# Second products gathered in six PSUM banks, the next pair's operands made in the first products, and the keys' maxima transposed behind the second products

## The chip, the cores and the metric

The kernel runs on 1 core of one Trainium2 chip. The metric is the device time of one execution in microseconds (us); the time given is the median of three runs.

## The reference, cut to what matters

```python
q_s = softmax of q over each row of 64          # 8 batches x 8 heads x 576 x 64
k_s = softmax of k over the sequence (axis 2)   # needs each column's maximum over 576 rows
kv  = einsum('bhsd,bhse->bhde', k_s, v)
x   = einsum('bhsd,bhde->bhse', q_s, kv)        # seen as 4608 tokens x 512
h   = x @ w_in                                  # 512 -> 2048
x   = (h * clip(h + 3, 0, 6) / 6) @ w_out       # first MLP, 2048 -> 512
h   = x @ w2_in
out = (h * sigmoid(h)) @ w2_out                 # second MLP, the same sizes
```

Everything is fp32. Each fp32 operand of a product is split into an upper and a lower fp32r part, and a product is the sum of three TensorE products (upper x upper, upper x lower, lower x upper).

## The kernel before, in words

The 4608 tokens are 9 blocks of 512 (NB). **Attention and the first MLP** run together, block by block. Each block has 16 steps (f = 0 to 15). A step `n` issues on TensorE `mm1(s)` (12 matmuls, the hidden block h), small attention matmuls, and `mm2(prev)` (12 matmuls of the step before). One attention unit (two heads of a block) begins every four steps and goes through stages 0 to 6; of its keys, stage 0 takes maxima over five row groups on VectorE (`k_max`, three instructions, L290 to L292), stage 1 transposes them on TensorE (`k_turn`, L297) and reduces them on VectorE (`k_peak`, L303), stage 2 spreads the result over the partitions (`k_spread`, L309). `q_load` brings the transposed queries back through DRAM (`zd`) on ScalarE's DMA queue. In these steps each engine works in the order in which the code emits; there is no scheduler.

**The second MLP** treats blocks 1 to 8 as four pairs (b = 0 to 3); block 0 is done at the very end with plain `mm1`/`mm2`. A pair is computed by a Strassen-like scheme with seven products P1 to P7 in place of eight, once for the *first products* (x times w2_in, function `inner`, L992) and once for the *second products* (gated hidden times w2_out, function `outer`, L1142). A unit is 6 matmuls of 128x128 by 512 columns. The first products of a pair are 56 units, P1 to P7 for each of 8 hidden pairs n, each hidden pair gathered in three PSUM banks A, B and C. The second products are 56 units too, product by product in the order of `KEYS`, 8 units (i = 0 to 7) each. Their moving operands come from the gated hidden tiles `g` and sums of them: GpSimd makes T1 and T3 while the first products run, and T2 and T4 while the second run (`next_t2`, `next_t4`); ScalarE takes the upper part (`split`, L1081), VectorE the lower (`split_low`, written by the helper at L979), `LOOK` = 4 units ahead into one of five rotating tile pairs (`split_tile`). `joins` adds the products into eight kept tiles `fixed`, from which `turn` transposes the output during the next pair's first products. Banks are handed out in rotation over eight (`bank`).

Two blocks' x operands for the next pair are prepared by `x_ahead`, in two column halves c: four loads of 256 KB from `yd`, sums on GpSimd, seven splits (`high` on ScalarE, `low` on VectorE) whose parts are stored to `xd`. `x_fetch` reads them back into the operand tiles during the second products. Weights come through six `ring` tiles of two units each, fetched six tiles ahead by `fetch` (L878).

The order of the second MLP is a table of events: `when(t, fn)` files a piece of code at time t, in units, and the pieces are emitted in the order of t. So t decides the place in each engine's queue, and nothing else: an engine runs the next instruction of its queue as soon as what it waits for is there.

Of the kernel before, what the change touches and what calls it, by code (L numbers as in the profile page):

```python
# [9 lines left out]
F32 = mybir.dt.float32  # L10
# [18 lines left out]
def efficient_attention_then_two_mlps(  # L29
# [47 lines left out]
    xd = dram.tile([2, 7, P, 2, 2, BLK], F32, name="xd")  # L77
# [80 lines left out]
    OUTER = ("A11", "S3", "S2", "S1", "S4", "A22", "A12")  # L158
# [800 lines left out]
    KEYS = ("P1", "P7", "P6", "P5", "P3", "P4", "P2")  # L959

    def second_mlp(last):
# [48 lines left out]
        def pair_events(b, n, t):  # L1010
# [37 lines left out]
            def t3():  # L1048
                add(op["spare"][:, n], g_of(2 * n + 1)[:, 1], g_of(2 * n)[:, 1],
                    ALU.subtract, nc.gpsimd)  # L1050
# [15 lines left out]
        def split_tile():  # L1066
            n = turns[0] % 5
# [29 lines left out]
        def x_ahead(j, c, side, t, step):  # L1097

            st = {n: op["spare"][:, 3 + m] for m, n in enumerate(("B12", "B22", "B11", "B21", "T"))}

            def load(n):
                jj, h = j + (n[2] == "2"), int(n[1] == "2")
                nc.sync.dma_start(st[n], yd[jj, 2 * h + c])

            def high(n, src):
                d["x", n] = split_tile()
                nc.scalar.copy(d["x", n][0], st[src])  # L1107

            def low(n, src):
                hi, lo = d.pop(("x", n))  # L1110
                add(lo, st[src], f32(hi), ALU.subtract)
                to = xd[side, XS.index(n)]
# [333 lines left out]
```

## Time and profile before

| | |
|---|---|
| median of 3 runs (lowest, highest) | 1659.18 us (1657.49, 1660.66) |
| the profiled execution: its time, its span | 1661.98 us, 1660.3 us |
| TensorE matmul busy | 1613.2 us, 97% |
| VectorE, ScalarE, GpSimd busy | 1075.3, 740.2, 422.4 us |
| DMA traffic, mean over the span | 317.61 MB, 191 GB/s |
| mean granted TensorE clock | 0.997 of full |

The span is the time from the first to the last instruction of the profiled execution; 1.68 us of the execution's time lie outside it. A TensorE matmul's busy time overlaps the next one's, so how long a run of matmuls takes is read from the starts.

### The profile page before, as it was taken

How to read it: one execution, taken by the hardware profiler on the slowest of the kernel's cores; microseconds unless marked ns; L12 is line 12 of the kernel's file. 1: busy time of each engine (PE TensorE's matmuls, PEld its weight loads, DVE VectorE, ACT ScalarE, POOL GpSimd, SP SyncE). 2: the span in 40 equal slices, each digit the busy share in tenths (PEclk: the TensorE clock that was granted, in tenths of full speed). 3: DMA queues.
4: the chain of work that ended last, by engine and by line, in shares of the span. 5: the costliest groups of instructions: out<-in, count | busy, mean ns of one | idle time of the engine just before them, and what ended most of it. 6: DMA issues, size and time to landing. Idle time of an engine off the chain costs nothing.

```text
span 1660.3 us, 22032 instructions
## 1 busy us (share of the span) xinstructions
PE 1613.2 (97%) x7612; PEld 1302.0 (78%) x7612; DVE 1075.3 (65%) x1737; ACT 740.2 (45%) x1306; POOL 422.4 (25%) x334
## 2 busy tenths in 40 slices
PE   6999999999999999999999899999999999999998
PEld 4777787787877788888888687788778878887887
DVE  8996666565666666555556568865976595569422
ACT  6885344343444444443434344444444443444322
POOL 2100111101111110111121456343724370345000
PEclk9999999999999999999999899999999999999999
DMA  8912434444543434443341977987899687669730
GB/s 252 337 35 67 132 105 140 123 137 130 168 122 106 138 116 141 129 138 98 93 161 58 335 285 282 361 310 237 297 349 310 222 302 256 216 213 356 241 127 26
DMA packets 291838, 317.61 MB, mean 191 GB/s; under 512 B 113424, under 2 KB 197392, under 8 KB 291728
## 3 DMA queue, kind: packets, MB, share of 16 engines
q1 hardware_dynamic: 228768, 300.97, 53.9%
q10 hardware_dynamic: 62960, 15.25, 4.1%
q8 instruction: 60, 0.98, 0.2%
q14 instruction: 50, 0.41, 0.1%
HBM read 234.62 MB, written 81.53 MB: 190 GB/s over the span
## 4 chain that ended last, share of the span: by engine, by line
PE 64%; DVE 17%; ACT 6%; DMA 6%; issue 4%; ACTq 3%; POOL 0%; SPq 0%; DVEq 0%; POOLq 0%
PE pb L992 17%; PE h L493 17%; PE y L563 14%; PE pb L1142 10%; DVE gsp L979 6%; ACTq L424 3%; PE y L565 2%; DMA zd<-qz 2%; DMA xd<-gsp 2%; DVE r L513 2%; PE pa L451 1%; ACT g L521 1%; ACT r L506 1%; DVE fa L128 1%; DVE fa L132 1%
## 5 line engine op out<-in xcount | busy, mean ns | idle before, releaser
L493 PE MATMUL h<-x,wi 128*128 128x512 f32 x1920 | 472.6, 393 | 2.4 <-DVE wi L153 1.0
L563 PE MATMUL y<-g,wo 128*128 128x512 f32 x1728 | 420.6, 392 | 0.0
L493 PEld LDWEIGHTS h<-x,wi 128*128 128x128 f32 x1920 | 356.6, 188 | 79.3 <-DVE wi L153 2.7
L563 PEld LDWEIGHTS y<-g,wo 128*128 128x128 f32 x1728 | 321.3, 188 | 67.0
L992 PE MATMUL pb<-xo,ring 128*128 128x512 f32 x1344 | 317.1, 394 | 8.4 <-DVE U L979 6.8
L1142 PE MATMUL pb<-gsp,ring 128*128 128x512 f32 x1344 | 316.5, 393 | 6.1 <-DVE gsp L979 3.4
L1142 PEld LDWEIGHTS pb<-gsp,ring 128*128 128x128 f32 x1344 | 249.6, 188 | 71.7 <-DVE gsp L979 18.1
L992 PEld LDWEIGHTS pb<-xo,ring 128*128 128x128 f32 x1344 | 252.3, 189 | 62.1 <-DVE U L979 7.2
L513 DVE SCALAR_TENSOR_TENSOR r<-r,h 128x512 f32<-128x512 f32 x128 | 88.0, 687 | 209.5 <-ACT r L506 204.5
L979 DVE TENSOR_TENSOR gsp<-g,gsp 128x512 fp32r<-128x512 f32 x192 | 169.3, 906 | 45.2 <-ACT gsp L1081 44.1
L1081 ACT CAST gsp<-g 128x512 fp32r<-128x512 f32 x192 | 115.3, 621 | 110.1 <-PE pb L1142 52.9
L506 ACT ACTIVATE r<-h 128x512 f32<-128x512 f32 x144 | 86.2, 599 | 152.5 <-PE h L493 133.7
L521 ACT CAST g<-r 128x512 fp32r<-128x512 f32 x144 | 89.5, 622 | 118.7 <-DVE r L513 106.6
L524 DVE TENSOR_TENSOR g<-r,g 128x512 fp32r<-128x512 f32 x144 | 103.9, 722 | 53.6 <-ACT g L521 43.8
L398 POOL TENSOR_TENSOR qe<-qe,qs 128x512 f32<-128x512 f32 x36 | 37.7, 1046 | 345.5 <-DVE qs L393 332.2
L979 DVE TENSOR_TENSOR g<-r,pb 128x512 f32<-128x512 f32 x96 | 65.6, 683 | 54.3 <-ACT r L1005 54.1
L979 DVE TENSOR_TENSOR gsp<-spare,gsp 128x512 fp32r<-128x512 f32 x74 | 83.9, 1163 | 18.0 <-ACT gsp L1107 18.0
L376 POOL TENSOR_TENSOR qe<-qraw,qm 128x512 f32<-128x512 f32 x34 | 36.0, 1060 | 215.1 <-DVE qm L368 139.4
L1005 ACT ACTIVATE r<-pb 128x512 f32<-128x512 f32 x96 | 57.1, 595 | 75.3 <-DVE pb L979 63.2
L979 POOL TENSOR_TENSOR s<-U,s 128x512 f32<-128x512 f32 x32 | 43.5, 1359 | 154.5 <-DVE U L979 83.3
L197 POOL TENSOR_TENSOR ws_sum<-fa 128x256 f32<-128x256 f32 x32 | 29.4, 920 | 163.7 <-ACT r L506 96.2
L354 ACT ACTIVATE kv<-pa,rs 64x64 fp32r<-64x64 f32 x56 | 17.3, 309 | 108.1 <-DMA qt<-zd 53.6
(152 smaller groups left out, 1640.0 us busy)
## 6 DMA issues: line engine op xcount, KB each, us to landing
ring<-ws SPq DMA_DIRECT2D x224, 512.0 KB, 4.9
ws<-sp SPq DMA_DIRECT2D x128, 256.0 KB, 2.5
xd<-gsp SPq DMA_DIRECT2D x84, 256.0 KB, 5.6
xo<-xd SPq DMA_DIRECT2D x42, 512.0 KB, 6.2
yd<-o SPq DMA_DIRECT2D x36, 256.0 KB, 2.4
wi_early<-in_moe_w_in_dram SPq DMA_DIRECT2D x16, 512.0 KB, 9.3
wo_early<-in_moe_w_out_dram SPq DMA_DIRECT2D x16, 512.0 KB, 9.6
wi_raw<-in_moe_w_in_dram SPq DMA_DIRECT2D x16, 512.0 KB, 4.2
```

What stands on the lines that cost most here:

```text
L424: nc.scalar.dma_start(t[b * 32 : b * 32 + 32].rearrange("i (c a k) -> i c a k", c=NCH, a=4), zb[b])
L493: nc.tensor.matmul(h, w[:, a, c, :], x[:, e, c, :], start=(c == 0 and n == 0), stop=(c == NC - 1 and n == 2),)
L506: nc.scalar.activation(self.r, self.h, AF.Relu, bias=3.0)
L513: nc.vector.scalar_tensor_tensor(out=r, in0=r, scalar=6.0, in1=h, op0=ALU.min, op1=ALU.mult)
L521: nc.scalar.copy(self.g[:, 0], self.r)
L524: nc.vector.tensor_tensor(out=self.g[:, 1], in0=self.r, in1=f32(self.g[:, 0]), op=ALU.subtract)
L563: nc.tensor.matmul(y[c], w[:, a, cs], g[:, e, :], start=st, stop=sp)
L979: (eng or nc.vector).tensor_tensor(out=out, in0=a, in1=b, op=how)
L992: nc.tensor.matmul(to, ws_[:, a], e[:, c], start=p in ("P1", "P6", "P5") and c == 0 and m == 0, stop=c == 1 and m == 2, skip_group_check=True,
L1005: nc.scalar.activation(r, d[b, n, key], AF.Sigmoid)
L1081: nc.scalar.copy(t[0], source(p, i))
L1142: nc.tensor.matmul(d[b, p][m], w[:, a, m * P : (m + 1) * P], t[e], start=i == 0 and k == 0, stop=i == NPR - 1 and k == 2, skip_group_check ...
```

## The change

Two moves stand in attention: `k_turn` goes from behind `mm1` to behind `mm2(prev)` of the same step, `k_peak` from the end of that step to the start of the next. In the second MLP the order of the products becomes P1, P5, P6, P2, P7, P3, P4; P2 is accumulated in P1's banks, P3 in P5's, P7 and P4 in P6's, so that six banks are taken where each product took two new ones, and `joins` copies three sums on ScalarE and adds five times per half on VectorE (before: one copy and seven additions). T1 and T2 are made in the first products, T3 and T4 in the second. `x_ahead` stands in the first products alone, stages its loads in the two `g` tiles in place of `spare`, and splits into three of the five tile pairs.

```diff
-    xd = dram.tile([2, 7, P, 2, 2, BLK], F32, name="xd")
+    xd = dram.tile([7, P, 2, 2, BLK], F32, name="xd")
...
-    OUTER = ("A11", "S3", "S2", "S1", "S4", "A22", "A12")
+    OUTER = ("A11", "S1", "S2", "A12", "S3", "S4", "A22")
...
-    KEYS = ("P1", "P7", "P6", "P5", "P3", "P4", "P2")
+    KEYS = ("P1", "P5", "P6", "P2", "P7", "P3", "P4")
...
             def t1():
                 g = g_of(2 * n)
                 add(g[:, 1], g[:, 1], g[:, 0], ALU.subtract, nc.gpsimd)
-            when(e["P3"] + 1.9, t3)
-            when(e["P3"] + 2.0, t1)
+            def t2():
+                add(op["spare"][:, n], g_of(2 * n + 1)[:, 1], g_of(2 * n)[:, 1],
+                    ALU.subtract, nc.gpsimd)
+            when(e["P3"] + 1.9, t1)
+            when(e["P3"] + 2.0, t2)
...
-                "P1": g1[:, 0], "P7": op["spare"][:, i], "P6": g1[:, 0], "P5": g1[:, 1],
-                "P3": g2[:, 1], "P4": g1[:, 0], "P2": g2[:, 0],
+                "P1": g1[:, 0], "P5": g1[:, 1], "P6": op["spare"][:, i], "P2": g2[:, 0],
+                "P7": g1[:, 0], "P3": g2[:, 1], "P4": g1[:, 1],
...
-        def split_tile():
-            n = turns[0] % 5
+        def split_tile(x=False):
+            n = 2 + turns[0] % 3 if x else turns[0] % 5
             turns[0] += 1
...
-        def next_t2(i):
+        def next_t3(i):
             g1 = g_of(2 * i)
-            add(g1[:, 0], op["spare"][:, i], g1[:, 0], ALU.add, nc.gpsimd)
+            add(g1[:, 0], op["spare"][:, i], g1[:, 0], ALU.subtract, nc.gpsimd)
 
         def next_t4(i):
-            g1 = g_of(2 * i)
-            add(g1[:, 0], g1[:, 0], g_of(2 * i + 1)[:, 0], ALU.subtract, nc.gpsimd)
+            add(g_of(2 * i)[:, 1], g_of(2 * i + 1)[:, 0], op["spare"][:, i], ALU.subtract, nc.gpsimd)
...
-        def x_ahead(j, c, side, t, step):
-
-            st = {n: op["spare"][:, 3 + m] for m, n in enumerate(("B12", "B22", "B11", "B21", "T"))}
+        def x_ahead(j, c, t, step):
+
+            st, hl = {}, {}
...
+                if n in ("B22", "B21"):
+                    pair = gs.tile([P, 2, BLK], F32, tag="g", name="xst")
+                    st[n], st[{"B22": "B12", "B21": "B11"}[n]] = pair[:, 0], pair[:, 1]
                 jj, h = j + (n[2] == "2"), int(n[1] == "2")
                 nc.sync.dma_start(st[n], yd[jj, 2 * h + c])
...
             def high(n, src):
-                d["x", n] = split_tile()
-                nc.scalar.copy(d["x", n][0], st[src])
+                hl[n] = split_tile(True)
+                nc.scalar.copy(hl[n][0], st[src])
 
...
-            def total(to, x, y, how):
-                add(st[to], st[x], st[y], how, nc.gpsimd)
-
-            for m, n in enumerate(("B22", "B12", "B11", "B21")):
+            def total(to, x, y):
+                add(st[to], st[x], st[y], ALU.subtract, nc.gpsimd)
+
+            for m, n in enumerate(("B22", "B12", "B21", "B11")):
                 when(t - 4.0 + 0.3 * m, lambda n=n: load(n))
-            when(t + 0.02, lambda: total("T", "B22", "B12", ALU.subtract))
-            when(t + 0.03, lambda: total("B12", "B12", "B11", ALU.subtract))
-            when(t + 3 * step + 0.02, lambda: total("T", "T", "B11", ALU.add))
-            when(t + 5 * step + 0.02, lambda: total("T", "B21", "T", ALU.subtract))
             for m, (n, src) in enumerate((
-                ("B22", "B22"), ("B11", "B11"), ("T3", "T"), ("T1", "B12"), ("T2", "T"),
-                ("B21", "B21"), ("T4", "T"),
+                ("B22", "B22"), ("B21", "B21"), ("T1", "B12"), ("T2", "B22"), ("B11", "B11"),
+                ("T4", "B21"), ("T3", "B11"),
             )):
                 when(t + m * step + 0.3, lambda n=n, src=src: high(n, src))
                 when(t + m * step + 0.9, lambda n=n, src=src: low(n, src))
-
-        def x_fetch(side, n, low):
-            nc.sync.dma_start(f32(op[n][low]), xd[side, XS.index(n)][:, low])
+            when(t + 0.02, lambda: total("B12", "B12", "B11"))
+            when(t + 1 * step + 0.25, lambda: total("B22", "B22", "B12"))
+            when(t + 3 * step + 0.25, lambda: total("B21", "B21", "B22"))
+            when(t + 4 * step + 1.0, lambda: total("B11", "B22", "B11"))
...
+            new = p in ("P1", "P5", "P6")
             if i == 0:
-                d[b, p] = [bank(), bank()]
+                d[b, p] = [bank(), bank()] if new else d[b, {"P2": "P1", "P3": "P5"}.get(p, "P6")]
...
-                        start=i == 0 and k == 0, stop=i == NPR - 1 and k == 2,
+                        start=new and i == 0 and k == 0, stop=i == NPR - 1 and k == 2,
...
+                one, two, three, four = fixed[4 * m : 4 * m + 4]
                 at = d[b, p][m]
-                if name == "one":
-                    nc.scalar.copy(one, at)
+                if name in ("s1", "s5", "C11"):
+                    nc.scalar.copy({"s1": one, "s5": three, "C11": four}[name], at)
...
-                    add(three, d[b, "P7"][m], two)
+                    d[b, "U3", m] = small("U3")
+                    add(d[b, "U3", m], at, one)
...
-                    add(c22, at, three)
-                elif name in ("U4", "C12"):
+                    add(three, d.pop((b, "U3", m)), three)
+                elif name == "C12":
                     add(two, at, two)
...
-                "P1": ("one",), "P7": (), "P6": ("U2", "U3"), "P5": ("C22", "U4"),
-                "P3": ("C12",), "P4": ("C21",), "P2": ("C11",),
+                "P1": ("s1",), "P5": ("s5",), "P6": ("U2",), "P2": ("C11",), "P7": ("U3", "C22"),
+                "P3": ("C12",), "P4": ("C21",),
...
-                    x = fixed[4 * m + ((0, 1), (2, 3))[a][h]]
+                    x = fixed[4 * m + ((3, 1), (0, 2))[a][h]]
...
-                    when(start[0] + 1.4 + 1.8 * i, lambda i=i: next_t2(i))
+                    when(start[0] + 6.4 + 3.0 * i, lambda i=i: next_t3(i))
                 if p == "P6":
-                    when(start[0] + 18.4 + 2.6 * i, lambda i=i: next_t4(i))
...
-                side = b % 2
-                if b == 0:
-                    x_ahead(j + 2, 0, side, t0 + 1.0, 1.8)
-                    x_ahead(j + 2, 1, side, t0 + 15.0, 1.8)
-                else:
-                    x_ahead(j + 2, 1, side, t0 + 4.0, 3.2)
-                if b + 2 < BB:
-                    x_ahead(j + 4, 0, 1 - side, start[0] + 22.0, 4.0)
+                x_ahead(j + 2, 0, t0 + 9.0, 3.2)
+                x_ahead(j + 2, 1, t0 + 31.0, 3.2)
...
-                    when(base + 15.3 + c, lambda c=c: load_y(0, c))
-                    when(base + 19.3 + 2 * c, lambda c=c: split_y(0, c))
+                    when(base + 44.3 + c, lambda c=c: load_y(0, c))
+                    when(base + 48.4 + 2 * c, lambda c=c: split_y(0, c))
...
+            if 2 in has_k:
+                k_peak(has_k[2])
...
             mm1(s)
             if 2 in has_k:
                 k_spread(has_k[2], a_pool)
-            if 1 in has_k:
-                k_turn(has_k[1], a_pool)
...
-            if 1 in has_k:
-                k_peak(has_k[1])
             if 0 in has_k:
                 k_max(has_k[0])
             mm2(prev)
+            if 1 in has_k:
+                k_turn(has_k[1], a_pool)
```

What moves on the engines, in the rows of the built programs:

TensorE in an attention step: `m_2338` is one unit's maxima, `h` the `mm1` of the step, `y` the `mm2` of the step before. Before the change:

```order
L563 MATMUL y_1687<-g,wo 128x512
L493 MATMUL h<-x,wi 128x512 x12
L297 MATMUL pa<-ident,m_2338 128x128
L563 MATMUL y_1684<-g,wo 128x512
L563 MATMUL y_1685<-g,wo 128x512
```

and with the change, in the same step:

```order
L563 MATMUL y_1685<-g,wo 128x512
L563 MATMUL y_1686<-g,wo 128x512
L563 MATMUL y_1687<-g,wo 128x512
L297 MATMUL pa<-ident,m_2338 128x128
L451 MATMUL pa<-qT,kv_91 128x4x32 x3
```

The transpose of the maxima now has the twelve `mm2` matmuls ahead of it.

ScalarE where the first MLP ends and the first pair begins: `s` is a copy of a first product's bank, `o` the first MLP's last block on its way to `yd`, `gsp` an operand of `x_ahead` being split. Before:

```order
L1017 COPY s_8192<-pb 128x512
L1107 CAST gsp<-spare 128x512
L572 ACTIVATE o<-y_7596 128x512
L572 ACTIVATE o<-y_7598 128x512
L1107 CAST gsp<-spare 128x512
L1023 COPY s_8241<-pb 128x512
L1005 ACT_TABLE_LOAD
```

and with the change:

```order
L1017 COPY s_8186<-pb 128x512
L572 ACTIVATE o<-y_7596 128x512
L572 ACTIVATE o<-y_7598 128x512
L1023 COPY s_8228<-pb 128x512
L1005 ACT_TABLE_LOAD
```

The two splits are gone from this place; VectorE's queue loses its two `low` halves there in the same way. The first split now stands behind the third sigmoid.

GpSimd at the second products of one pair (the last), from the last of the eight sums of the first burst on. Before (T2 of pair 6 and 7, then T4 of pairs 0 to 2; each waits for what the brackets name):

```order
L979 TENSOR_TENSOR g_8780<-spare,g_8780 128x512 [waits DVE_49]
L979 TENSOR_TENSOR g_8862<-spare,g_8862 128x512 [waits DVE_49,Pool_49]
L979 TENSOR_TENSOR g_8255<-g_8255,g_8296 128x512 [waits DVE_49]
L979 TENSOR_TENSOR g_8356<-g_8356,g_8396 128x512 [waits DVE_49]
L979 TENSOR_TENSOR g_8450<-g_8450,g_8492 128x512 [waits DVE_49]
```

and with the change (T3 of pair 6, T4 of pair 0, T3 of pair 7, T4 of pairs 1 and 2):

```order
L979 TENSOR_TENSOR g_8776<-spare,g_8776 128x512 [waits DVE_49]
L979 TENSOR_TENSOR g_8239<-g_8278,spare 128x512 [waits DVE_49]
L979 TENSOR_TENSOR g_8868<-spare,g_8868 128x512 [waits Pool_49]
L979 TENSOR_TENSOR g_8326<-g_8366,spare 128x512 [waits DVE_49]
L979 TENSOR_TENSOR g_8414<-g_8453,spare 128x512 [waits DVE_49]
```

Both bursts are still eight sums each. T4 overwrote the operand of P6, whose `split_low` it waited for (units 16 to 23); it now overwrites that of P5 (units 8 to 15).

## Rows read from the trace of the kernel before

**Rows 1.** The page: busy time by engine, and one DMA issue (KB each, us to landing).

```profile
PE 1613.2 (97%) x7612; PEld 1302.0 (78%) x7612; DVE 1075.3 (65%) x1737; ACT 740.2 (45%) x1306; POOL 422.4 (25%) x334
...
xd<-gsp SPq DMA_DIRECT2D x84, 256.0 KB, 5.6
```

**Rows 2.** Waits over the span: us in total, times, longest.

```profile
PE pa L297 <- DVE m L292: 7.4, 18, 1.0
```

**Rows 3.** TensorE in the chain that ended last: start, us, what.

```profile
738.01 2.72 PE y L563 x12
```

**Rows 4.** Timeline of one attention step: start, us, instruction, idle time before it.

```profile
306.94 2.88 PE L493 MATMUL h<-x,wi 128*128 128x512 f32 x12
...
309.03 0.69 DVE L524 TENSOR_TENSOR g<-r,g 128x512 fp32r<-128x512 f32 x1 [0.19 <-ACT g L521]
...
310.42 0.29 DVE L292 TENSOR_TENSOR m<-m,kbuf 128x128 f32<-128x128 f32 x1
...
310.86 0.30 PE L297 MATMUL pa<-ident,m 128*128 128x128 f32 x1 [1.04 <-DVE m L292]
```

**Rows 5.** Timeline between the two MLPs, without TensorE.

```profile
914.50 1.94 SPq L878 DMA_DIRECT2D ring<-ws  x4
916.48 2.36 SPq L1103 DMA_DIRECT2D spare<-yd  x4
924.04 0.62 ACT L1107 CAST gsp<-spare 128x512 fp32r<-128x512 f32 x1 [9.78 <-DMA spare<-yd]
...
925.30 1.28 DVE L574 TENSOR_SCALAR o<-y 128x512 f32<-128x512 f32 x2
...
926.50 0.68 DVE L979 TENSOR_TENSOR U<-pb,s 128x512 f32<-128x512 f32 x1
...
929.59 1.28 ACT L1005 ACT_TABLE_LOAD   x1 [2.95 <-DMA yd<-o]
930.88 0.60 ACT L1005 ACTIVATE r<-pb 128x512 f32<-128x512 f32 x1
...
931.51 0.69 DVE L979 TENSOR_TENSOR g<-r,pb 128x512 f32<-128x512 f32 x1 [3.11 <-ACT r L1005]
```

**Rows 6.** Timeline of TensorE alone, there and behind it.

```profile
917.56 2.88 PE L992 MATMUL pb<-xo,ring 128*128 128x512 f32 x12
...
927.24 7.94 PE L992 MATMUL pb<-xo,ring 128*128 128x512 f32 x21 [6.80 <-DVE U L979]
...
951.51 9.84 PE L992 MATMUL pb<-xo,ring 128*128 128x512 f32 x42 [0.69 <-ACT s L1023]
962.22 3.02 PE L992 MATMUL pb<-xo,ring 128*128 128x512 f32 x12 [0.88 <-ACT s L1023]
```

**Rows 7.** Stretches: length, busy of PE, PEld, DVE, ACT, POOL; clock, DMA share, GB/s.

```profile
923.00:934.00 11.00, 6.76 (x17) 5.32 (x18) 6.20 (x9) 4.98 (x8) 4.04 (x3) 0.53 0.95 334
...
1114.00:1124.00 10.00, 10.00 (x48) 8.26 (x47) 7.38 (x11) 4.50 (x8) 5.89 (x5) 1.00 1.04 372
```

**Rows 8.** Timeline of GpSimd in the third pair's second products.

```profile
1333.96 11.94 POOL L979 TENSOR_TENSOR g<-spare,g 128x512 f32<-128x512 f32 x7
1348.34 13.57 POOL L979 TENSOR_TENSOR g<-g,g 128x512 f32<-128x512 f32 x8 [2.44 <-DVE gsp L979]
```

**Rows 9.** Timeline of VectorE in the same stretch.

```profile
1347.58 16.09 DVE L979 TENSOR_TENSOR gsp<-g,gsp 128x512 fp32r<-128x512 f32 x12
```

**Rows 10.** Timeline of TensorE where second products begin or end.

```profile
1001.80 1.52 PE L1142 MATMUL pb<-gsp,ring 128*128 128x512 f32 x6
...
1246.62 3.56 PE L992 MATMUL pb<-xo,ring 128*128 128x512 f32 x15
...
1325.37 1.52 PE L1142 MATMUL pb<-gsp,ring 128*128 128x512 f32 x6
...
1404.89 3.34 PE L992 MATMUL pb<-xo,ring 128*128 128x512 f32 x14
...
1564.80 2.88 PE L493 MATMUL h<-x,wi 128*128 128x512 f32 x12
```

More of the change, by code (lines that the diff above doesn't have):

```diff
@@ L1047, in pair_events @@
             when(e["P4"] + 1.25, lambda: mul(b, n, "B", 1, 0))
-            def t3():
-                add(op["spare"][:, n], g_of(2 * n + 1)[:, 1], g_of(2 * n)[:, 1],
-                    ALU.subtract, nc.gpsimd)
             def t1():
@@ L1105, in high @@
             def high(n, src):
[L1106 to L1107 removed]
+                hl[n] = split_tile(True)
+                nc.scalar.copy(hl[n][0], st[src])
             def low(n, src):
[L1110 removed]
+                hi, lo = hl.pop(n)
                 add(lo, st[src], f32(hi), ALU.subtract)
[L1112 removed]
+                to = xd[XS.index(n)]
                 nc.sync.dma_start(to[:, 0, c], f32(hi))
                 nc.sync.dma_start(to[:, 1, c], f32(lo))
[L1116 to L1119 removed]
+            def total(to, x, y):
+                add(st[to], st[x], st[y], ALU.subtract, nc.gpsimd)
+            for m, n in enumerate(("B22", "B12", "B21", "B11")):
                 when(t - 4.0 + 0.3 * m, lambda n=n: load(n))
[L1121 to L1124 removed]
             for m, (n, src) in enumerate((
[L1126 to L1127 removed]
+                ("B22", "B22"), ("B21", "B21"), ("T1", "B12"), ("T2", "B22"), ("B11", "B11"),
+                ("T4", "B21"), ("T3", "B11"),
             )):
@@ L1130, in x_ahead, with x_fetch @@
                 when(t + m * step + 0.9, lambda n=n, src=src: low(n, src))
-        def x_fetch(side, n, low):
-            nc.sync.dma_start(f32(op[n][low]), xd[side, XS.index(n)][:, low])
+            when(t + 0.02, lambda: total("B12", "B12", "B11"))
+            when(t + 1 * step + 0.25, lambda: total("B22", "B22", "B12"))
+            when(t + 3 * step + 0.25, lambda: total("B21", "B21", "B22"))
+            when(t + 4 * step + 1.0, lambda: total("B11", "B22", "B11"))
+        def x_fetch(n, low):
+            nc.sync.dma_start(f32(op[n][low]), xd[XS.index(n)][:, low])
         def outer(b, p, i):
@@ L1148, in joins @@
         def joins(b, p, t):
-            def tile(m, n):
-                return fixed[4 * m + n]
             def do(m, name):
-                one, two, three, c22 = fixed[4 * m : 4 * m + 4]
+                one, two, three, four = fixed[4 * m : 4 * m + 4]
                 at = d[b, p][m]
-                if name == "one":
-                    nc.scalar.copy(one, at)
+                if name in ("s1", "s5", "C11"):
+                    nc.scalar.copy({"s1": one, "s5": three, "C11": four}[name], at)
                 elif name == "U2":
@@ L1160, in do @@
                 elif name == "U3":
-                    add(three, d[b, "P7"][m], two)
+                    d[b, "U3", m] = small("U3")
+                    add(d[b, "U3", m], at, one)
                 elif name == "C22":
-                    add(c22, at, three)
-                elif name in ("U4", "C12"):
+                    add(three, d.pop((b, "U3", m)), three)
+                elif name == "C12":
                     add(two, at, two)
-                elif name == "C21":
-                    add(three, three, at, ALU.subtract)
                 else:
@@ L1224, in second_mlp @@
                 if p == "P1":
-                    when(start[0] + 1.4 + 1.8 * i, lambda i=i: next_t2(i))
+                    when(start[0] + 6.4 + 3.0 * i, lambda i=i: next_t3(i))
                 if p == "P6":
-                    when(start[0] + 18.4 + 2.6 * i, lambda i=i: next_t4(i))
+                    when(start[0] + 26.4 + 2.8 * i, lambda i=i: next_t4(i))
                 when(t, lambda b=b, p=p, i=i: outer(b, p, i))
@@ L1246, in second_mlp @@
                             start[0] + 3.1 + 6.0 * m + 3.0 * low,
-                            lambda n=n, low=low, side=side: x_fetch(side, n, low),
+                            lambda n=n, low=low: x_fetch(n, low),
                         )
```

## The prediction

> **What bounds the kernel now.** The page's first part is read first: TensorE is busy for 97% of the span [rows 1], so the time can only change where TensorE waits, or where its clock falls. How long a matmul takes comes from the chain: twelve start within 2.72 us [rows 3], which is 0.227 us each, and a unit of six takes 1.36 us. In the timeline the same twelve are shown for 2.88 us [rows 4], because the last is drawn past its slot; an idle time shown in front of a matmul is therefore 0.16 us short, and I add that.
>
> The waits come next. The attention's transposes of the maxima wait 18 times for VectorE, 7.4 us together, at most 1.0 [rows 2]. One step shows why: `mm1` starts at 306.94 and its slots end at 309.66, but the third maximum ends only at 310.71, and the transpose stands ahead of `mm2` [rows 4]. The largest single wait is between the two MLPs: the twelve matmuls of 917.56 end at 920.28, the next start at 927.24 [rows 6]. ScalarE had stopped for 9.78 us at a split whose load was not there; the copies `o` of the first MLP's last block, and VectorE's first `U`, stand behind such splits in their queues [rows 5]. In the 11 us from 923 the granted clock is 0.53 of full, so it was at 1.2 GHz for nearly all of it, and TensorE had just been idle [rows 7].
>
> The second products are read from their starts. From the first pair's to the third pair's first products are 244.82 us; one stretch of first products, 1246.62 to 1325.37, takes 78.75; the two second products in between therefore take 166.07 [rows 10]. With the last P4 of the first kind, one such stretch is 57 units, 77.52 us, so these two lose 11.0 us. The third pair's (1325.37 to 1404.89) loses 2.0, the last pair's (159.91 - 78.75 = 81.16) loses 3.6 [rows 10]. Together 16.7 us. The third pair has nothing but its own work there, so 2.0 is the part that every pair has.
>
> **The change, part by part.** *The transposes.* Behind `mm2` a transpose comes 2.72 us later than now, and the longest wait is 1.0 + 0.16 us, so all 18 should go: 7.4 + 18 x 0.16 = 10.3 us. `mm2` does not inherit the wait: its g is there at 309.72 in the step shown, against 309.66 for its first slot, and its last four matmuls alone use that half [rows 4]. `k_peak` now leads VectorE's next step; `k_spread` stands behind a whole `mm1` (2.72 us) and needs only that one short reduction. I cost the new places at nothing. What hides them is these twelve matmuls; if they did not, 10.3 us would be back.
>
> *Between the MLPs.* Without the two splits ahead, ScalarE and VectorE copy `o` as soon as the last `mm2` ends, and `U` follows ahead of 920.28. The wait goes, 6.96 us, and with it the slow clock: 21 matmuls are shown in 7.94 us [rows 6], the last of them drawn for 0.39; the other 20 took 0.378 us each, against 0.227, 3.0 us too long. Together 10.0 us. What is late next is the first sigmoid. Now it waits 2.95 us for a store of `o` [rows 5], whose staging tile it reuses. With the change that store is issued near 917.8 (last `mm2` round plus a copy), where a load issued at 916.48 stands now, behind the same four ring fetches, and that load landed at about 924.0 [rows 5]. From there: table load 1.28, sigmoid 0.60, product 0.69, and a `U` of 0.68 [rows 5] that must have read its bank before P4 writes it. That is 927.3; P4's slot, six units behind the end of `mm2` at 917.56, is at 925.7. Loss 1.6, and something for the copy behind it: I take 2.0, between 0 (the store lands sooner) and 3.0 (as it waits now). The Trainium skill, "DMA: Bandwidth & Descriptors", section "Queues, rings and completion order", says that on each DMA engine one queue's descriptors are consumed in ring order; by that the store cannot overtake the fetches and 2.0 stands, without it the sum would be 2.0 us better.
>
> *The operands of the next pair.* The first pair's first products lose 0.69 + 0.88 + 2 x 0.16 = 1.9 us more at 951.51 and 962.22, behind ScalarE [rows 6], with seven splits per 1.8 x 7 units on five tile pairs: a tile came back into use after 1.8 x 5 x 1.36 = 12.2 us. That loss I count as gone. Now a tile returns after 3.2 x 3 x 1.36 = 13.1 us, of which a store needs 5.6 to land [rows 1]; the first products get both halves, the outputs and the ring, in stretches where the DMA engines are already full (1.04) with one half [rows 7]. I price that at 0.5 us for each of three first products, 1.5, between 0 and the 1.9 of today's worst.
>
> *The second products.* GpSimd and VectorE take turns: seven sums in 11.94 us and eight in 13.57 [rows 8] are 1.70 each, and VectorE's lower halves then go at that pitch. TensorE wants one per 1.36 us, and so loses 0.34 per sum once VectorE has no lead. Today there are two bursts, of seven in a row and eight, and 2.44 us of idle GpSimd between them, because T4 waits for P6's first split [rows 8]. In that gap VectorE is fast: its 12 splits from 1347.58 take 16.09 us [rows 9], of which eight at 1.70 are 13.6, so four take 2.5, while TensorE uses 5.4; the lead of 2.9 pays for the second burst (8 x 0.34 = 2.7). The first burst costs 7 x 0.34 = 2.4, and 2.0 is what is lost. With the change T4 waits for P5's splits, which VectorE makes during the first burst, and the first T4 is queued ahead of the last T3. The later numbers in the event table do not hold GpSimd back. So the gap closes: 16 sums in a row, 16 x 0.34 = 5.4, less the lead of 0.4 that shows today and up to 0.7 more, since one sum fewer is queued ahead and delays VectorE by one split less: 4.3 to 5.0, I take 4.7 per pair, 18.8 for four, 2.1 more than now. Bounds: 2.0 per pair (8.0) and 5.4 (21.6). What today's first two pairs lose to splits for the next pair, and the last to `split_y`, is gone within these 4.7. The rows alone would also allow that bursts beyond the first cost nothing, as the second does today. The Trainium skill, "SBUF — State Buffer", section "Who interferes with whom", says that a VectorE instruction with two SBUF inputs and a GpSimd one that reads SBUF exclude each other for a whole instruction; by that it is 18.8, by the second burst alone 8.0.
>
> *The joins.* Per pair four additions less on VectorE and four copies more on ScalarE, all behind the bursts or on an engine with 45% busy [rows 1]; banks accumulate sums that were copied units before. Nothing, and if the cover were gone, four times 0.68 us.
>
> **The sum.** -10.3 - 10.0 + 2.0 - 1.9 + 1.5 + 2.1 = -16.6 us. The profiled execution took 1661.98 us, 2.8 above the median of the runs, so 1645.4 there and 1642.5 as a median.
>
> **The rivals.** *The gap stays or costs nothing* (10%): the bursts lose 2.0 per pair; 10.8 us better, 1631.7. For it speaks that the new events are filed later, and that the second burst is free today; against it GpSimd's waits, which name P5's splits. *Late tiles* (13%): three tile pairs and full DMA engines make ScalarE wait in both halves, 3.8 us per first products in place of 0.5: 9.9 worse, 1652.4. For it the waits of [rows 6], against it the pitch of 3.2 units, with which the later pairs' halves lose nothing now (78.75 us [rows 10] is 55 units, 74.8, and 32 output transposes). *The transposes gain nothing* (4%): the wait comes back at `k_spread` or in VectorE's queue; 10.3 worse, 1652.8. *Slower* (6%): the loads of the second half reuse a staging tile that the first half's last split, filed 1.5 units later, still reads. They hold SP's queue, and ring fetches stand behind them. A ring tile is fetched five tiles, 13.6 us, ahead of its use, and a load can take 7.6 (916.48 to 924.04, [rows 5]): once SP is held for over 6.0 us, TensorE stops and the clock falls, as between the MLPs. At 10.0 us for each of three first products, in place of the 0.5, that is 28.5 worse: 1671. Against it: 1.5 units are 2.0 us.
>
> **How the numbers follow.** My forecast holds 67%. The range 1634 to 1653 takes in late tiles and the lost gain of the transposes and leaves out the first rival and the slower one. Within 0.2% (3.3 us), about what a measurement of this kernel tells from no change, lies little: 3%. Faster 91%, slower 6%.
>
> **What would show it.** In the profile after: no wait of a transpose for a maximum; no gap above 3 us between the MLPs and a full clock there; GpSimd's sums of the second products in one run of 16 at 1.70, with 82 us from a pair's second products to the next first ones; first products of 79 to 80 us. I am wrong if GpSimd pauses between T3 and T4, if ScalarE waits for stores to `xd` in the first products, or if ring fetches land late.

## The result, and the profile after

The changed kernel takes 1645.08 us (median of four runs, 1644.69 to 1645.35), the kernel before 1659.91 (1657.49 to 1660.66) in the same comparison: a ratio of 0.9913, 95% interval 0.9896 to 0.993. Its profiled execution takes 1645.06 us with a span of 1643.3, against 1661.98 and 1660.3. So the profiled executions differ by 16.9 us, the medians by 14.8.

The page after: busy time, and the stores of split operands (KB each, us to landing). Beside [rows 1]:

```profile
PE 1611.2 (98%) x7612; PEld 1301.1 (79%) x7612; DVE 1082.1 (66%) x1721; ACT 748.6 (46%) x1322; POOL 422.4 (26%) x334
...
xd<-gsp SPq DMA_DIRECT2D x84, 256.0 KB, 6.1
```

TensorE's matmuls are the same and 2 us less busy; what went is idle time. Where it went is read from the starts of the stages. Timeline of TensorE alone after, at the stages' borders (start, us, instruction, idle time before it); L1145 is `outer`, L1142 before:

```profile
904.75 8.32 PE L992 MATMUL pb<-xo,ring 128*128 128x512 f32 x36
915.36 64.59 PE L992 MATMUL pb<-xo,ring 128*128 128x512 f32 x282 [2.29 <-DVE U L979]
979.78 1.52 PE L1145 MATMUL pb<-gsp,ring 128*128 128x512 f32 x6
...
1061.48 1.30 PE L992 MATMUL pb<-xo,ring 128*128 128x512 f32 x5
...
1142.06 2.63 PE L992 MATMUL pb<-xo,ring 128*128 128x512 f32 x6 [3.01 <-ACT s L1023]
1144.49 2.18 PE L1145 MATMUL pb<-gsp,ring 128*128 128x512 f32 x6
...
1226.08 2.20 PE L992 MATMUL pb<-xo,ring 128*128 128x512 f32 x9
...
1304.89 1.53 PE L1145 MATMUL pb<-gsp,ring 128*128 128x512 f32 x6
...
1387.33 1.98 PE L992 MATMUL pb<-xo,ring 128*128 128x512 f32 x8
...
1466.10 1.52 PE L1145 MATMUL pb<-gsp,ring 128*128 128x512 f32 x6
...
1547.78 2.43 PE L493 MATMUL h<-x,wi 128*128 128x512 f32 x10
```

| stage | before | after | difference | forecast |
|---|---|---|---|---|
| up to the end of the first MLP (917.56 [rows 6]; 904.75) | 917.56 | 904.75 | -12.8 | -10.3 |
| first products, first pair (to 1001.80 [rows 10]; 979.78) | 84.24 | 75.03 | -9.2 | -9.4 |
| first products, second pair (before: the third's 78.75 [rows 10]) | 78.75 | 83.01 | +4.3 | +0.5 |
| first products, third pair | 78.75 | 78.81 | +0.1 | +0.5 |
| second products, four pairs, above 77.52 each | 16.7 | 17.3 | +0.6 | +2.1 |
| behind them, to the end of the span | 95.5 | 95.5 | 0.0 | 0.0 |

The losses of the second products are 4.2, 4.1, 4.9 and 4.2 us (81.70, 81.59, 82.44 and 81.68, less 77.52). The forecast of the second line is -10.0 + 2.0 - 1.9 + 0.5. The lines sum to -17.0, against -16.6 forecast. The fourth pair's first products, which prepare no operands, take 78.75 us before and 78.77 after.

The attention step of [rows 4] after the change, all engines, part of it:

```profile
306.13 2.89 PE L563 MATMUL y<-g,wo 128*128 128x512 f32 x12
...
306.76 0.29 DVE L292 TENSOR_TENSOR m<-m,kbuf 128x128 f32<-128x128 f32 x1
...
308.86 0.27 PE L297 MATMUL pa<-ident,m 128*128 128x128 f32 x1
...
308.88 1.02 PE L451 MATMUL pa<-qT,kv 128*128 128x192 f32 x6
309.17 0.29 DVE L303 TENSOR_REDUCE mx<-pa 128x1 f32<-128x128 f32 x1
...
309.74 2.92 PE L493 MATMUL h<-x,wi 128*128 128x512 f32 x12
```

The third maximum ends at 307.05, and the transpose starts 1.8 us later, without a wait. The row of [rows 2] is gone from the waits, and `k_peak` follows the transpose at once.

Between the MLPs after, without TensorE (beside [rows 5]):

```profile
904.49 1.09 ACT L572 ACTIVATE o<-y 128x512 f32<-128x512 f32 x2 [3.04 <-PE y L563]
...
904.99 2.32 SPq L575 DMA_DIRECT2D yd<-o  x4
905.47 0.68 DVE L979 TENSOR_TENSOR U<-pb,s 128x512 f32<-128x512 f32 x1
...
912.09 1.28 ACT L1005 ACT_TABLE_LOAD   x1 [5.19 <-DMA yd<-o]
...
914.62 0.68 DVE L979 TENSOR_TENSOR U<-pb,s 128x512 f32<-128x512 f32 x1
```

`o` is copied as soon as `mm2` ends, and the first `U` with it. The sigmoid's table load then waits 5.19 us for a store of `o`, and the second `U` is late by it: the 2.29 us in front of 915.36. The first store of `o`, issued at 904.99, landed at 911.69, behind the four ring fetches issued ahead of it, which landed from 905.66 to 910.97; the order of issue was the order of landing, as the prediction had assumed.

GpSimd and VectorE in the third pair's second products after (two timelines; beside [rows 8, 9]):

```profile
1313.36 11.93 POOL L979 TENSOR_TENSOR g<-spare,g 128x512 f32<-128x512 f32 x7
1325.26 1.74 POOL L979 TENSOR_TENSOR g<-g,spare 128x512 f32<-128x512 f32 x1
1326.95 1.74 POOL L979 TENSOR_TENSOR g<-spare,g 128x512 f32<-128x512 f32 x1
1328.65 11.92 POOL L979 TENSOR_TENSOR g<-g,spare 128x512 f32<-128x512 f32 x7
```

```profile
1312.76 16.48 DVE L979 TENSOR_TENSOR gsp<-g,gsp 128x512 fp32r<-128x512 f32 x10
1329.16 12.57 DVE L979 TENSOR_TENSOR gsp<-spare,gsp 128x512 fp32r<-128x512 f32 x8
1341.65 2.49 DVE L979 TENSOR_TENSOR gsp<-g,gsp 128x512 fp32r<-128x512 f32 x4
```

From 1313.36 to 1340.57 sixteen sums follow each other without a pause, 1.70 us each. VectorE's splits come no faster until the last sum is done; then four take 2.49 us.

The end of the second pair's first products after: ScalarE's timeline, SP's, and two stretches (length, busy of PE, PEld, DVE, ACT, POOL; clock, DMA share, GB/s):

```profile
1133.52 0.63 ACT L1109 CAST gsp<-xst 128x512 fp32r<-128x512 f32 x1
1140.42 0.62 ACT L1081 CAST gsp<-g 128x512 fp32r<-128x512 f32 x1 [6.27 <-DMA xd<-gsp]
```

```profile
1137.30 0.33 SPq L1116 DMA_DIRECT2D xd<-gsp  x1
```

```profile
1131.00:1141.00 10.00, 8.05 (x36) 6.35 (x34) 4.78 (x6) 2.69 (x6) 3.59 (x3) 1.00 1.01 362
1142.40:1145.80 3.40, 3.40 (x10) 2.62 (x9) 2.77 (x6) 1.65 (x4) 0.73 (x1) 0.51 0.14 54
```

The last split for the next pair is at 1133.52; its lower part, which VectorE ends at 1137.28, is stored from 1137.30. ScalarE's next instruction is the first split of the second products, and it waits 6.27 us for that store, since it was given the same tile pair. `x_ahead` takes its tiles from three of the five and the second products from all five, with one counter for both: here turn 83 gives 2 + 83 % 3 = 4, and turn 84 gives 84 % 5 = 4. The sigmoids and copies of the first products stand behind it on ScalarE. TensorE idles 3.2 us, and the granted clock behind that is 0.51 of full, the level of 1.2 GHz. In the third pair turns 152 and 154 share tile 4 as well: ScalarE waits 2.9 us for the store there, and TensorE loses nothing by it (78.81 us).

### The profile page after: what moved, and what is told of

The parts are those of the page before. It is cut to its first block, busy times and chain, and to the rows that moved or that the text cites. A ratio compares the mean times of both kernels' runs of the same rounds, so it can differ in the third digit from the quotient of the medians.

```text
span 1643.3 us, 21988 instructions
## 1 busy us (share of the span) xinstructions
PE 1611.2 (98%) x7612; PEld 1301.1 (79%) x7612; DVE 1082.1 (66%) x1721; ACT 748.6 (46%) x1322; POOL 422.4 (26%) x334
## 4 chain that ended last, share of the span: by engine, by line
PE 84%; DVE 11%; DMA 2%; ACT 2%; issue 1%; POOL 1%; SPq 0%; ACTq 0%; DVEq 0%; POOLq 0%
PE h L493 25%; PE y L563 22%; PE pb L992 16%; PE pb L1145 13%; DVE gsp L979 5%; PE y L565 3%; PE pa L451 2%; PE pa L337 1%; DVE fa L132 1%; DVE fa L128 1%; PE pb L1185 1%; DMA ring<-ws 1%; DMA xd<-gsp 0%; DMA xst<-yd 0%; DVE fa L121 0%
## 5 line engine op out<-in xcount | busy, mean ns | idle before, releaser
L493 PE MATMUL h<-x,wi 128*128 128x512 f32 x1920 | 472.6, 394 | 2.3 <-DVE wi L153 1.0
L493 PEld LDWEIGHTS h<-x,wi 128*128 128x128 f32 x1920 | 356.5, 188 | 78.7 <-DVE wi L153 2.4
L563 PE MATMUL y<-g,wo 128*128 128x512 f32 x1728 | 418.1, 391 | 0.0
L563 PEld LDWEIGHTS y<-g,wo 128*128 128x128 f32 x1728 | 322.4, 188 | 68.1
L1145 PE MATMUL pb<-gsp,ring 128*128 128x512 f32 x1344 | 321.2, 395 | 1.9
L992 PE MATMUL pb<-xo,ring 128*128 128x512 f32 x1344 | 315.5, 393 | 5.3 <-ACT s L1023 3.0
L1145 PEld LDWEIGHTS pb<-gsp,ring 128*128 128x128 f32 x1344 | 248.9, 188 | 73.2 <-DVE gsp L979 23.2
L992 PEld LDWEIGHTS pb<-xo,ring 128*128 128x128 f32 x1344 | 250.7, 188 | 58.6 <-ACT s L1023 3.4
L979 DVE TENSOR_TENSOR gsp<-g,gsp 128x512 fp32r<-128x512 f32 x192 | 174.4, 928 | 61.5 <-ACT gsp L1081 58.2
L354 ACT ACTIVATE kv<-pa,rs 64x64 fp32r<-64x64 f32 x56 | 17.3, 309 | 109.7 <-DMA qt<-zd 55.2
L979 POOL TENSOR_TENSOR g<-g 128x512 f32<-128x512 f32 x32 | 42.9, 1341 | 64.4 <-DVE g L979 64.4
```

Source lines behind the costliest of these rows:

```text
L493: nc.tensor.matmul(h, w[:, a, c, :], x[:, e, c, :], start=(c == 0 and n == 0), stop=(c == NC - 1 and n == 2),)
L563: nc.tensor.matmul(y[c], w[:, a, cs], g[:, e, :], start=st, stop=sp)
L979: (eng or nc.vector).tensor_tensor(out=out, in0=a, in1=b, op=how)
L992: nc.tensor.matmul(to, ws_[:, a], e[:, c], start=p in ("P1", "P6", "P5") and c == 0 and m == 0, stop=c == 1 and m == 2, skip_group_check=True,
L1145: nc.tensor.matmul(d[b, p][m], w[:, a, m * P : (m + 1) * P], t[e], start=new and i == 0 and k == 0, stop=i == NPR - 1 and k == 2, skip_gro ...
```

## The experiments

Edits are to the changed kernel where nothing else is said. The kernel before took 1663.05 to 1663.27 us (medians) on the chips of these runs, and the changed kernel 1644.79 on the chip of the last four, so times of the edited ones are set against 1644.8 to 1645.1.

### The attention moves alone

The kernel before with `k_turn` behind `mm2(prev)` and `k_peak` at the head of the next step, and nothing else of the change.

> The kernel before with the attention moves alone: the transposes of the maxima behind the second products, the second MLP as it was. Theory (the waits go whole): 10.3 us of waits go, and 2.0 us more, since the first matmul behind each of these 23 transposes starts 0.09 us late in the trace of before and no longer does in the changed kernel: about 1647.5 from 1659.9, and no wait of TensorE for the maxima. Rival (part of the changed kernel's 12.8 us by this point of the program comes from the second MLP's side): 4 to 9 us.

Measured: 1649.45 us, ratio 0.9918 (0.9905 to 0.9932), 13.6 us below the kernel before on that chip. The waits for maxima are gone, as in the changed kernel, and the first products begin at 899.50 us, there at 899.30. So the first line of the table is all of this move's. It is 2.5 us more than the 18 waits.

The expectation put 2.0 us of that down to late starts, and that is too much. Counted from start to start in the traces of this run and of before, the waits come to 10.5 us. The late starts do go from `mm2`: the second of a run of 512-column matmuls right behind a 128-column transpose starts 0.09 us late, of 48 such starts at L563 before 25 are left, and `mm2`'s starts are 2.5 us shorter in all. But 22 of the moved transposes now have attention's narrow matmuls (L451) behind them, and these start late in place of `mm2`'s. TensorE in the step of [rows 4], before:

```profile
313.74 0.94 PE L451 MATMUL pa<-qT,kv 128*128 128x192 f32 x6
314.52 2.91 PE L493 MATMUL h<-x,wi 128*128 128x512 f32 x12
```

From the first L451 to `mm1` it is 0.78 us, and 0.86 in the step after the change shown above. Over the 22 steps 1.6 us come back that way. The transposes' own slots are 0.65 us shorter, so the new place is worth some 1.5 us besides the waits. What remains, some 0.6 us, is spread over the stage and has no cause shown.

### The loads of the first pair's operands later, in the kernel before

```diff
-                    x_ahead(j + 2, 0, side, t0 + 1.0, 1.8)
-                    x_ahead(j + 2, 1, side, t0 + 15.0, 1.8)
+                    x_ahead(j + 2, 0, side, t0 + 6.0, 1.8)
+                    x_ahead(j + 2, 1, side, t0 + 20.0, 1.8)
```

> The kernel before with one edit: the first pair's two x_ahead stretches begin five units later (6.0 and 20.0 in place of 1.0 and 15.0), so the two splits no longer stand ahead of the copies of the first MLP's last block. Theory (the queue order at this place is the cause): the wait of 6.96 us and the 3.0 us of slow clock go, and 2.4 us come back as the wait of the first hidden pair's U behind the store of o, as in the changed kernel: about 7.5 us faster, 1652.4. Rival (the ring fetches or the stores are late themselves, whatever stands in the queues): under 3 us faster.

Measured: 1659.84 us, ratio 0.9983 (0.9975 to 0.9992), 3.2 below the kernel before on that chip, where 7.5 were expected. TensorE's timeline there:

```profile
918.53 8.32 PE L992 MATMUL pb<-xo,ring 128*128 128x512 f32 x36
928.72 7.36 PE L992 MATMUL pb<-xo,ring 128*128 128x512 f32 x24 [1.87 <-DVE U L979]
937.57 16.66 PE L992 MATMUL pb<-xo,ring 128*128 128x512 f32 x72 [1.50 <-ACT s L1023]
...
961.30 39.73 PE L992 MATMUL pb<-xo,ring 128*128 128x512 f32 x174 [2.32 <-ACT s L1023]
```

The long wait of [rows 6] goes from 6.80 to 1.87 us with nothing changed but the place of `x_ahead`'s work: it was that work, queued ahead of `o`. The edit moves the loads and the splits together, so that it was the splits is read from the queues [rows 5] and not shown by itself. But most of the gain is given back. The splits, still one per 1.8 units, now meet the sigmoids, and the waits behind ScalarE grow from 0.69 and 0.88 [rows 6] to 1.50, 0.98 and 2.32. The clock still falls for a part, to a mean of 0.86 from 928 to 940 us. So the -10.0 and the -1.9 of the forecast were not independent: with the narrow pitch, starting later saves the one and adds to the other. The wider pitch by itself was not run.

### The tile order

```diff
-            n = 2 + turns[0] % 3 if x else turns[0] % 5
+            n = 2 + (turns[0] % 70 + 1) % 3 if x else (turns[0] + 1) % 5
```

> The changed kernel with the rotation of the split tiles renumbered, so that the first splits of the second products take the two g tiles and the tile that x_ahead used last comes fifth. Theory (an accident of counting: in the second pair the last x split and the first split of the second products fall on the same tile, turn 83 and 84, and ScalarE waits 6.3 us for its stores): the second pair's first products take 78.8 us in place of 83.0, 4.2 us faster, 1640.9. Rival (DMA is full there, stores land late and some wait comes whatever the tile): within 1 us of the changed kernel, 1645.1.

Measured: 1642.20 us, ratio 0.9877 (0.9863 to 0.989), 2.6 to 2.9 below the changed kernel, where 4.2 were expected. TensorE:

```profile
1063.44 2.88 PE L992 MATMUL pb<-xo,ring 128*128 128x512 f32 x12
...
1142.21 1.52 PE L1145 MATMUL pb<-gsp,ring 128*128 128x512 f32 x6
```

The second pair's first products take 78.77 us in place of 83.01, with the same loads, stores and pitch. So the loss was the one meeting of two turns at one tile, and neither the number of tiles nor the full DMA engines. The whole kernel gains less than that, mainly because two earlier stages came out longer in this run: the first MLP ends at 905.74 (904.75), and the first pair's first products take 75.99 us (75.03). There the granted clock was 0.66 of full from 916 to 921 us, behind a wait of 2.01 us that the edit leaves alone; in the changed kernel it had stayed at 1.00 behind 2.29.

### T4 into the tiles of T2

```diff
-            add(g_of(2 * i)[:, 1], g_of(2 * i + 1)[:, 0], op["spare"][:, i], ALU.subtract, nc.gpsimd)
+            add(op["spare"][:, i], g_of(2 * i + 1)[:, 0], op["spare"][:, i], ALU.subtract, nc.gpsimd)
...
-                "P7": g1[:, 0], "P3": g2[:, 1], "P4": g1[:, 1],
+                "P7": g1[:, 0], "P3": g2[:, 1], "P4": op["spare"][:, i],
...
-                    when(base + 48.4 + 2 * c, lambda c=c: split_y(0, c))
+                    when(base + 51.8 + 0.8 * c, lambda c=c: split_y(0, c))
```

The same sums; T4 now overwrites the operand of P6, so that it must wait for P6's splits, as before the change.

> The changed kernel with T4 written over T2's place (where P6's operand lies) in place of T1's (P5's); so each T4 again waits for P6's split, and the splits of y come a little later (51.8 + 0.8 c in place of 48.4 + 2 c). Theory (GpSimd's 16 sums in a row are the price, a pause between two bursts of 8 gives VectorE its lead back): the second products lose 2.0 to 2.5 us per pair in place of 4.1 to 4.9, 7 to 9 us faster in all, 1636 to 1638. Rival (the number of sums counts, not the pause): within 1 us of the changed kernel, 1645.1.

Measured: 1633.16 us, ratio 0.9821 (0.9808 to 0.9834), some 12 below the changed kernel, more than the 7 to 9 expected. GpSimd in the third pair's second products:

```profile
1307.57 11.94 POOL L979 TENSOR_TENSOR g<-spare,g 128x512 f32<-128x512 f32 x7
1322.00 1.61 POOL L979 TENSOR_TENSOR spare<-g,spare 128x512 f32<-128x512 f32 x1 [2.50 <-DVE gsp L979]
...
1325.28 11.95 POOL L979 TENSOR_TENSOR spare<-g,spare 128x512 f32<-128x512 f32 x7
```

A pause of 2.50 us is back, and the second products lose 1.2, 1.8, 1.9 and 1.2 us, 6.1 in all in place of 17.3. That is less than the 2.0 per pair that the third pair lost before with its 2.44 us [rows 8], and with the tiles renumbered too (three edits, below) every pair loses 1.2; why less than before is not settled.

### No T3 and T4 at all

The eight `next_t3` and eight `next_t4` of each pair are left out, so P7 and P4 multiply other operands of the same shape.

> The changed kernel without the sums T3 and T4 in the second products (P7 and P4 multiply the hidden tiles as they lie), which leaves out part of the computation. Theory (the alternation of GpSimd and VectorE is the whole loss of the second products): each pair's second products fall from 81.6-82.4 us to within 0.5 of 77.5, about 17 us faster, 1628. Rival (part of the loss is TensorE waiting for ScalarE's copies or for tiles): 80 us and more remain.

Measured: 1629.87 us, ratio 0.9801 (0.9787 to 0.9815), 15 below, where 17 were expected. VectorE in the third pair's second products:

```profile
1319.60 0.69 DVE L979 TENSOR_TENSOR gsp<-spare,gsp 128x512 fp32r<-128x512 f32 x1 [0.67 <-ACT gsp L1081]
```

Each split takes 0.69 us and VectorE has 0.67 to spare in each unit. The second products of the first, third and fourth pair take 77.52 us, 57 units to the hundredth; the second's take 79.21, beginning at half clock behind the tile met above. So all of the loss but that 1.7 us is the bursts', and joins and shared banks cost nothing.

### Tiles of its own for the last `o`

```diff
+        own = None
+        if (ph, j) == (0, NB - 1):
+            two = att.tile([P, 2, 512], F32, tag="qT", bufs=1, name="o")
+            own = [two[:, 0], two[:, 1]] + [
+                att.tile([P, 512], F32, tag=tag, bufs=1, name="o") for tag in ("ke", "qe")
+            ]
...
-            o = tmp.tile([P, 512], F32, tag="t2k", name="o")
+            o = own[c] if own else tmp.tile([P, 512], F32, tag="t2k", name="o")
```

> The changed kernel with the first MLP's last four output tiles o in memory of their own (three tiles of the attention, free there) in place of the six rotating ones. Theory (the first sigmoid waits for the store of o, whose tile it reuses, and that wait is the 2.4 us left between the MLPs): the gap of 2.29 us in the first pair goes, 2.4 us faster, 1642.7. Rival (the ring fetches behind the stores are late too, or the wait moves to the next tile): under 1 us faster.

Measured: 1642.24 us, ratio 0.9876 (0.9862 to 0.9889), 2.6 to 2.8 below. TensorE and ScalarE (six lines of code more, so L998 is L992):

```profile
905.04 72.64 PE L998 MATMUL pb<-xo,ring 128*128 128x512 f32 x318
```

```profile
907.20 1.28 ACT L1011 ACT_TABLE_LOAD   x1
```

The table load no longer waits, and 318 matmuls run without a gap. The residue of 2.0 us in the forecast was the reused staging tile and nothing else.

### The spread behind the second products, first try

`k_spread` goes behind `mm2` as well, and `k_sub` ahead of `k_exp` in the next step.

> The changed kernel with the spreading transposes of the maxima (k_spread) also moved behind the second products, and k_sub to the start of the next step. Theory (a short transpose right ahead of the second products delays their first matmul by 0.09 us, and ahead of the first products it does not): 22 of the remaining 23 such delays go, 2.0 us faster, 1643.1. Rival (the delay follows the transpose wherever it stands, or k_sub's later place delays the exponential): no gain, or a loss of up to 5 us.

Measured: 1700.97 us, ratio 1.0232 (1.0212 to 1.0251). My edit put `k_sub` behind the load that refills its key tile, so it takes the next unit's keys, and waits for them:

```profile
DVE ke L317 <- DMA kbuf<-in_k_dram: 68.6, 10, 7.2
```

That says nothing of the place of `k_spread`. The run of all four edits has the same flaw.

> The changed kernel with the four edits together: tile rotation renumbered, T4 over T2's place, own tiles for o, k_spread behind the second products. If the four causes are separate, the gains add: 4.2 + 8 + 2.4 + 2.0 = 16.6 us, 1628.5. If one loss hides behind another (the second products' pause needs the lead that the tile wait gives), 3 to 6 us less.

Measured: 1681.55 us, ratio 1.0115 (1.0098 to 1.0132). Its second MLP has nothing of that: 78.7 us for each second products and 78.8 to 78.9 for the later first products.

### The changed kernel again, and the spread with the load behind it

> The changed kernel once more, on the chip of the three below, as their yardstick. Expected: a ratio of 0.991 to the kernel before, as in the first comparison, whatever the chip's own level; the same stages: 866.8 us of attention and first MLP, 80.5 of first products of the first pair, 83.0 for the second pair, 81.6 to 82.4 for each second products.

Measured: 1644.79 us, ratio 0.9889 (0.9876 to 0.9903). The stages repeat: 83.26 us for the second pair's first products, 81.6 to 82.0 for each second products. The changed kernel's level is that of the first comparison; it is the kernel before that is 3 us higher on this chip. What in it depends on the chip was not looked for.

```diff
+            if 3 in has_k and ("pb", has_k[3]) in live:
+                k_sub(has_k[3])
             if 3 in has_k and has_k[3] + 2 < NU:
                 load_k(has_k[3] + 2)
...
             mm1(s)
-            if 2 in has_k:
-                k_spread(has_k[2], a_pool)
...
-            if 2 in has_k:
-                k_sub(has_k[2])
...
                 k_turn(has_k[1], a_pool)
+            if 2 in has_k:
+                k_spread(has_k[2], a_pool)
```

> As spread_behind, but k_sub of the unit stands ahead of the load that refills its key tile. If the 0.09 us that the first matmul behind a transpose takes longer is all that the place of k_spread costs, the 23 that are left go too: 2.0 us below the changed kernel, and L563's matmuls show no more late starts in attention. If spread_behind was slow because of the place and not because its k_sub waited for the refilled tile: near 1701 again. Rival between them: k_sub now opens VectorE's step and delays its work for the gate, some us slower than the changed kernel.

Measured: 1645.19 us, ratio 0.9893 (0.988 to 0.9907): no gain. The first MLP ends at 904.34 us, 0.2 earlier than in the changed kernel run again. TensorE in one unit:

```profile
312.10 2.88 PE L563 MATMUL y<-g,wo 128*128 128x512 f32 x12
314.82 0.27 PE L309 MATMUL pa<-ident,mx 128*128 128x128 f32 x1
314.85 2.98 PE L493 MATMUL h<-x,wi 128*128 128x512 f32 x12
```

The twelve `mm2` are clean now, and the twelve `mm1` behind the transpose show 2.98 us. In both kernels 27 transposes L309 have wide matmuls right behind them, and these lose 0.09 us each, 2.4 us; in the changed kernel 25 of them at L563, here 25 at L493. My reading of the first experiment, that a transpose ahead of `mm2` costs this, was too narrow: any run of 512-column matmuls pays it, and `mm2` was rid of `k_turn`'s because L451 stands behind it now and loses 0.08 us in its place.

### Three and four edits together

> The edits of tile_order, t4_in_spare and own_tiles together. If their three costs are separate ones, they add up: 4.2 us of the second pair's first products, 12.6 of the four second products (81.6 to 82.4 each become 78.7) and 2.9 of the first pair's first products, 19.8 us below the changed kernel on the same chip, a span near 1623.5. Rival, VectorE is late in any case and the waits only move: little more than t4_in_spare alone, a span near 1631.

Measured: 1626.09 us, ratio 0.9775 (0.9761 to 0.9788), 18.7 below the changed kernel on the same chip. Its longest waits, and TensorE at three borders:

```profile
PE ph L297 <- DVE m L292: 8.3, 3, 7.3
PE h L536 <- ACT g L521: 2.4, 4, 0.7
```

```profile
905.25 72.42 PE L998 MATMUL pb<-xo,ring 128*128 128x512 f32 x318
977.50 1.52 PE L1151 MATMUL pb<-gsp,ring 128*128 128x512 f32 x6
...
1056.22 4.02 PE L998 MATMUL pb<-xo,ring 128*128 128x512 f32 x17
```

Against the changed kernel run again the costs add up: 12.1 us less in the second products (78.7 each), 4.5 in the second pair's first products, 2.4 in the first pair's, 19.0 together where 19.8 were expected. No wait of the second MLP is left among the longest. This version beats both kernels.

> The edits of three_edits and spread_after together: 21.8 us below the changed kernel, a span near 1621.5, if both hold; as three_edits, or some us more, if the place of k_spread gives nothing or costs.

Measured: 1625.40 us, ratio 0.9772 (0.9759 to 0.9786): the same as three edits within their spread.

## Why the prediction was right, point by point

**The total.** The sum, -16.6 us against the profiled execution, came out as -16.9. The predicted median is 2.6 us too low because of the 2.8 us that I took off for the profiled execution of before standing above its median; the changed kernel's profiled execution stands at its median. That the sum came so close is luck: two of its terms were off by 2.5 and 3.8 us, with opposite signs, and a third by 1.5.

**The transposes.** The mechanism was right, and shown by the moves alone. The size was not: -12.8 where I had -10.3. The waits came to 10.5 us. I had costed the new places at nothing, and they are worth 1.5: twelve `mm2` behind a transpose take 2.99 us in the timeline of before, others 2.88, and behind the move L451 gives back a part of that.

**Between the MLPs.** Right in both parts: the 6.80 us and the slow clock are gone, and the sigmoid's wait for the store of `o` is what comes next, 2.29 + 0.16 us where I had 2.0. That it is the staging tile is shown by the edit that gives `o` its own. But with the old pitch most of the gain is given back, as the later loads showed, and the clock was not safe: at the same wait it fell in two of the edited runs (last section).

**The operands of the next pair.** The mis-sized term: +0.5 for each of three first products, and the second's lost 4.3. The reason I gave for a loss, stores not landed within a tile's 13.1 us, did not occur inside a half. A sign of being wrong that I had named did show, ScalarE waiting for a store to `xd`, at another place: I had looked at each rotation by itself and not at the border, where the one ends and the other begins. By the code, turn 83 and turn 84 take the same tile. A split whose tile is still to be stored waits for VectorE's lower half and for the landing, here 3.2 and 3.1 us of the 6.27 and a store's median 5.6 [rows 1], so the code and that row would have shown several us at stake. The rival *late tiles* has a loss of this size, but three times and inside the halves.

**The second products.** Right: the pause closes, sixteen sums stand in a row at 1.70 us, in all four pairs, and the loss is 4.1 to 4.9 us per pair where I took 4.7 out of 4.3 to 5.0; three of the four lie just below that. Bringing the pause back takes 11.2 of the 17.3 us away, taking the sums away takes all but 1.7. The Trainium skill, "SBUF — State Buffer", section "Who interferes with whom", has a VectorE instruction with two SBUF inputs and a GpSimd one that reads SBUF exclude each other for a whole instruction. The traces agree: VectorE's split takes 0.69 us with the sums gone, and beside them the two engines get through one split and one sum per 1.70 us.

**The joins.** Nothing, as forecast: 77.52 us without the sums is 57 units.

**The rivals.** The pause did not stay, the wait did not come back at `k_spread`, and no wait of TensorE names a ring fetch: its two gaps in the second MLP name VectorE and ScalarE. What the slower rival starts from did occur: SP's queue waited once per pair for VectorE's split of the reused staging tile, 3.2, 3.2 and 3.8 us, below the 6.0 that it needed.

## What to carry to other kernels

Where two engines take turns, look at what lets the one off the path go: which tile a sum overwrites decided whether its burst came with a pause or without, and that was worth 11 us, while the six banks and the joins moved nothing. Where one rotation of buffers feeds two streams, look at the turn where they meet. And a profiled execution's distance from its median belongs to that kernel: add the forecast difference to the median only with that distance as part of the range.

## What the runs showed of the hardware

The second of a run of 512-column matmuls starts 0.09 us late behind a 128-column transpose (0.32 us behind the first in place of 0.23): so at 27 transposes L309, 2.4 us, and at 24 places of the second MLP behind output transposes. Behind L337's matmuls of 65 columns it is 0.11. A run of twelve behind L451's takes 0.03 us longer (2.92, others 2.88). L451's own run behind a transpose takes 0.08 us longer (0.86 in place of 0.78), so that moving the transpose from `mm2` to there saved little.

An idle TensorE of 3.2 us was followed by a granted clock of 0.51 of full; behind 2.45 us (in front of 915.36) it stayed at 1.00. But behind 2.17 us at the same place it was 0.66 from 916 to 921 us in the run of the tile order, and behind 2.18 us 0.57 from 915 to 919 in the run with the spread behind `mm2` and the load behind `k_sub`. So the length of the idle time alone did not decide it.

The kernel before ran at 1659.9 us in the first comparison and at 1663.1 to 1663.3 in three later ones, while the changed one kept its level (1645.1, 1644.8); why is open.
